# Attention beside a gated MLP in float32, one core: VectorE's low parts issued at the end of a step, and x prepared with longer distances

## The chip, the cores and the metric

The kernel runs on one core of a Trainium2 chip. A core has a matrix engine (PE, TensorE; its weight loads are listed apart as PEld), a vector engine (DVE, VectorE), a scalar engine (ACT, ScalarE), a general one (POOL, GpSimd), and SP, whose queue issues nearly all DMAs here. Each engine runs its own instructions in the order in which they are written; engines wait for each other by semaphores. The metric is the device time of one execution in microseconds (us). Before the change it was 1987.51 and 1981.97 us in two runs, with a median of 1984.74 us.

## The reference

```python
xn = layernorm(x)                                    # x: 2048 x 512
# A: attention, 32 heads of 128; the last 512 entries of the caches are used
q = xn @ wq                                          # 512 x 4096
p = softmax(q @ k^T * 128**-0.5)                     # 2048 x 512 for each head
s = concat(p @ v) @ wo                               # 4096 x 512
# B: gated MLP with a product over the sequence
z = gelu(xn @ w_in); z1, z2 = halves of z            # 688 columns each
g = silu((z1 * (w_sp @ layernorm(z2) + b_sp)) @ w_out)
out = x + s * g
```

Everything is float32. The kernel makes every product of two float32 matrices from three products of a rounded type: each operand is cut into a high part (a cast) and a low part (the operand minus its high part), and high x high, high x low and low x high are summed.

## The kernel before, in words

**Attention.** A block is one head times 512 rows of x; there are 128 blocks of 4 steps each, so 512 steps (`NSTEP`), and step `t` handles 128 rows. Around step `t` the main loop writes, for several blocks at once, a software pipeline:

- `score(t)`: three matmuls into a PSUM tile of 512 columns (`ps_3`, four buffers, shared with `outp`), its row maximum on DVE (`nm`, L439) and the exponential on ACT (`prob`, L441);
- `turn(t-1)`: DVE turns 32 x 32 blocks of `prob` (`pB`, L449), and SP stores the result to `p_dram`. After four of them `turned` reads them back in turned order as `pL`;
- `shares(t-10)`: the high part of P^T on ACT (`pT_h`, L466), its low part on POOL (`pT_l`);
- `pv(t-12)`: three matmuls of P and V. After the fourth of a block, `pv_out` makes `oT_h` on ACT and `oT_l` on DVE;
- `outp(t-17)`: three matmuls with wo, added to the rows' sums by DVE (`sacc`, L494);
- two or three of 42 matmuls per 16 steps that make q for the next four blocks (L413). They are seven products in the manner of Strassen, on quarters of 256 columns. `q_sum` forms sums of weights on POOL; `q_split` makes the high part on ACT (L395) and the low part on POOL for three of the seven and on DVE for four. High and low part go to a ring of four entries (`wring`, an `x8` tile, shown as x). `q_evict` and `q_done` take the results from PSUM, and `q_out` makes `qT_h` and `qT_l`.

**x.** The second half of the rows is prepared while the first is worked on. `later_x(p)` for p = 0 to 3 loads two tiles of 128 rows (`rawx`, five buffers), normalises them on DVE (`ln_stats`, `ln_apply`), turns them on PE, and makes eight pieces of 256 columns: four quarters and four sums of quarters (`T1` to `T4`). Of each, ACT makes the high and DVE or POOL the low part, and SP stores both to `x_dram` (`part`, L269). `fetch_x` reads them back before they are needed, as eight transfers of 1 MB. `t_sums` and `t_split` do the same for the first half in the steps -3 to 1.

**Order.** The order is the order of the program, written out by the main loop; nothing is reordered. Within a step it is: the loads due; `shares`; what the table `todo` has for this step (`plan`'s weight pieces, `q_sum` and `q_split`, `later_x`); `score`; the q products; `pv`; `outp`; `q_events` (`q_evict`, `q_done`); `pv_out`; `turned`; `turn`; and what `ends` has. So DVE's part of a step reads: low parts of `q_split` and `part`, `nm`, `sacc`, then `qs` and `qT_l` where due, `oT_l` where due, `pB`. The helper `rest` writes all low parts, which is why they share the line L59:

```python
def rest(engine, lo, whole, hi):
    engine.tensor_tensor(lo, whole, hi.bitcast(F32), op=OP.subtract)
...
for n, f in enumerate(f for p in range(4) for f in later_x(p)):
    at(30 + 5 * n // 2, f)
```

The last two lines put the 18 entries of each `later_x(p)` into `todo`, five steps for two entries, from step 30 to step 207. After the attention come the z products, layernorm, and the product over the sequence with the output (about the last 380 us of the span).

Of the kernel before, what the change touches and what calls it, by code (L numbers as in the profile page):

```python
# [8 lines left out]
F32 = mybir.dt.float32  # L9
# [3 lines left out]
OP = mybir.AluOpType  # L13
# [27 lines left out]
def mixer_kernel(ctx: ExitStack, tc: tile.TileContext, x, wh, w_in, w_sp, b_sp, w_out, out):  # L41
# [16 lines left out]
    def rest(engine, lo, whole, hi):  # L58
        engine.tensor_tensor(lo, whole, hi.bitcast(F32), op=OP.subtract)  # L59

# [160 lines left out]

    def t_sums(p):
# [27 lines left out]
    def later_x(p):  # L250
# [13 lines left out]
        def part(k, src, engine):  # L264
            st = xq.tile([P, 512], F32R, name="rawx")
            hi, lo = st[:, :256], st[:, 256:]
            nc.scalar.copy(hi, src())
            rest(engine, lo, src(), hi)
            nc.sync.dma_start(xd[1, k][:, :, :, p * P:(p + 1) * P],  # L269
                              st.bitcast(F32).rearrange("p (a c q) -> p a c q", a=2, q=P))  # L270
# [7 lines left out]
        def new_sums():  # L278
# [4 lines left out]
        vec, gp = nc.vector, nc.gpsimd  # L283
        return [load,
                lambda: ln_stats([t[a], t[b]], 100 * (p + 1)),
                lambda: ln_apply(t[a], 100 * (p + 1)),
                lambda: ln_apply(t[b], 100 * (p + 1) + 1),
                lambda: turned_copy(a),
                lambda: turned_copy(b),
                new_sums,  # L290
                lambda: part((0, 0), half(a, 0), vec),
                lambda: sub(half("u", 1)(), half(b, 1)(), half("u", 0)()),
                lambda: part((0, 1), half(b, 0), vec),
                lambda: part((1, 0), half(a, 1), gp),
                lambda: sub(half(b, 0)(), half(b, 1)(), half(b, 0)()),
                lambda: part((1, 1), half(b, 1), vec),
                lambda: sub(half(a, 1)(), half(a, 1)(), half("u", 1)()),
                lambda: part("T1", half("u", 0), gp),
                lambda: part("T2", half("u", 1), vec),
                lambda: part("T3", half(b, 0), gp),  # L300
# [655 lines left out]
```

## Time and profile before

| | |
|---|---|
| Time, median of two runs | 1984.74 us |
| The profiled execution's own time | 1983.97 us |
| Its span on the core | 1982.1 us |
| Mean granted TensorE clock | 0.986 |
| Busy: PE, DVE, POOL, ACT | 94%, 75%, 64%, 59% |
| HBM traffic over the span | 216 GB/s |

Rows of the profile that group instructions read: line, engine, operation, output<-inputs with the program's names (buffer numbers left out, so `ps_3` is ps), shapes and count | busy us in total, mean ns of one | idle time of the engine just before them in us, and what ended most of it. Rows of a timeline begin with the start and the duration in us and may end in square brackets with the idle time before them. A row of waits reads: who, waited for whom: us in total, times, longest. Rows of windows give the window's length, then busy us and instructions of PE, PEld, DVE, ACT and POOL, then the granted clock, the mean busy share of the 16 DMA engines, and GB/s.

### The profile page before, as it was taken

How to read it: one execution, taken by the hardware profiler on the slowest of the kernel's cores; microseconds unless marked ns; L12 is line 12 of the kernel's file. 1: busy time of each engine (PE TensorE's matmuls, PEld its weight loads, DVE VectorE, ACT ScalarE, POOL GpSimd, SP SyncE). 2: the span in 40 equal slices, each digit the busy share in tenths (PEclk: the TensorE clock that was granted, in tenths of full speed). 3: DMA queues.
4: the chain of work that ended last, by engine and by line, in shares of the span. 5: the costliest groups of instructions: out<-in, count | busy, mean ns of one | idle time of the engine just before them, and what ended most of it. 6: DMA issues, size and time to landing. Idle time of an engine off the chain costs nothing.

```text
span 1982.1 us, 28951 instructions
## 1 busy us (share of the span) xinstructions
PE 1860.5 (94%) x8658; PEld 1537.5 (78%) x8658; DVE 1484.3 (75%) x2427; ACT 1174.1 (59%) x2627; POOL 1264.1 (64%) x1127
## 2 busy tenths in 40 slices
PE   8888989989889899999999999999999999999999
PEld 7766767767667677677777777777777799999998
DVE  5678888888888788788888888888888756434333
ACT  4655656656666666666666666676666644334332
POOL 3576868878777787777888887888788626000000
PEclk9999999999999999999999999999999999999999
DMA  5698988988988899999989989989889961655442
GB/s 173 182 272 205 244 226 218 239 234 220 237 225 222 212 231 265 311 265 236 234 237 226 238 227 230 243 231 228 237 223 249 261 205 51 203 168 164 151 147 92
DMA packets 442542, 429.23 MB, mean 217 GB/s; under 512 B 26032, under 2 KB 318640, under 8 KB 440336
## 3 DMA queue, kind: packets, MB, share of 16 engines
q1 hardware_dynamic: 437776, 421.74, 79.0%
q10 hardware_dynamic: 4608, 5.64, 0.8%
q8 instruction: 68, 1.11, 0.2%
q14 instruction: 90, 0.74, 0.1%
HBM read 260.55 MB, written 166.72 MB: 216 GB/s over the span
## 4 chain that ended last, share of the span: by engine, by line
PE 36%; ACT 20%; DVE 17%; DMA 11%; issue 10%; POOL 4%; SPq 1%; ACTq 0%; DVEq 0%; POOLq 0%
ACT prob L441 8%; DVE nm L439 6%; ACT pT_h L466 4%; DMA pL<-p_dram 4%; PE ps_g L64 4%; PE ps_g L63 4%; PE ps_g L65 4%; DVE pB L449 4%; PE ps L63 3%; PE ps L65 3%; PE ps L64 3%; PE ps_a L413 3%; PE ps_a L64 3%; PE ps_a L63 3%; PE ps_a L65 3%
## 5 line engine op out<-in xcount | busy, mean ns | idle before, releaser
L59 POOL TENSOR_TENSOR pT_l<-pL,pT_h 128x512 fp32r<-128x512 f32 x507 | 670.7, 1323 | 266.9 <-ACT pT_h L466 244.5
L441 ACT ACTIVATE prob<-ps,nm 128x512 f32<-128x512 f32 x512 | 352.7, 689 | 504.0 <-DVE nm L439 502.7
L413 PE MATMUL ps_a<-x,x 128*128 128x512 f32 x1302 | 383.5, 395 | 0.5 <-DVE oT_l L59 0.3
L494 DVE SCALAR_TENSOR_TENSOR sacc<-ps,sums,sacc 128x512 f32<-128x512 f32 x496 | 363.4, 733 | 17.7 <-PE ps L65 16.6
L449 DVE STREAM_TRANSPOSE pB<-prob 128x512 f32<-128x512 f32 x512 | 357.4, 698 | 10.0 <-DMA p_dram<-pB 8.3
L439 DVE TENSOR_REDUCE nm<-ps 128x1 f32<-128x512 f32 x512 | 337.1, 658 | 3.1 <-PE ps L65 3.0
L466 ACT CAST pT_h<-pL 128x512 fp32r<-128x512 f32 x512 | 317.3, 620 | 23.7 <-DMA pL<-p_dram 10.6
L63 PE MATMUL ps<-wh,qT_h 128*128 128x512 f32 x512 | 221.8, 433 | 97.5 <-DVE sacc L494 92.3
L413 PEld LDWEIGHTS ps_a<-x,x 128*128 128x128 f32 x1302 | 247.7, 190 | 57.0 <-DVE oT_l L59 1.9
L59 POOL TENSOR_TENSOR wl<-raw,wh 128x512 fp32r<-128x512 f32 x192 | 251.6, 1311 | 8.7 <-ACT wh L139 8.7
L63 PEld LDWEIGHTS ps<-wh,qT_h 128*128 128x128 f32 x512 | 96.6, 189 | 180.6 <-DVE sacc L494 155.9
L64 PE MATMUL ps_a<-pT_l,wh 128*128 128x512 f32 x512 | 203.0, 397 | 4.0 <-POOL pT_l L59 3.9
L63 PE MATMUL ps_a<-pT_h,wh 128*128 128x512 f32 x512 | 202.1, 395 | 2.0 <-ACT pT_h L466 2.0
L65 PE MATMUL ps<-wh,qT_l 128*128 128x512 f32 x512 | 202.4, 395 | 0.0
L64 PE MATMUL ps<-wl,qT_h 128*128 128x512 f32 x512 | 202.3, 395 | 0.0
L63 PE MATMUL ps<-wh,oT_h 128*128 128x512 f32 x512 | 200.9, 392 | 0.7 <-DVE sacc L494 0.6
L65 PE MATMUL ps_a<-pT_h,wl 128*128 128x512 f32 x512 | 201.3, 393 | 0.0
L64 PE MATMUL ps<-wl,oT_h 128*128 128x512 f32 x512 | 200.0, 391 | 0.0
L65 PE MATMUL ps<-wh,oT_l 128*128 128x512 f32 x512 | 199.7, 390 | 0.0
L63 PE MATMUL ps_g<-z_h,x 128*128 128x344 f32 x512 | 162.2, 317 | 0.5 <-ACT z L719 0.5
L64 PE MATMUL ps_g<-z_l,x 128*128 128x344 f32 x512 | 162.1, 317 | 0.4 <-POOL z_l L59 0.4
L65 PE MATMUL ps_g<-z_h,x 128*128 128x344 f32 x512 | 161.9, 316 | 0.0
(197 smaller groups left out, 3342.6 us busy)
## 6 DMA issues: line engine op xcount, KB each, us to landing
p_dram<-pB SPq DMA_DIRECT2D x512, 256.0 KB, 5.1
pL<-p_dram SPq DMA_DIRECT2D x512, 256.0 KB, 5.6
raw<-wh SPq DMA_DIRECT2D x194, 256.0 KB, 5.0
wq<-wh SPq DMA_DIRECT2D x62, 256.0 KB, 6.2
x<-w_sp SPq DMA_DIRECT2D x60, 256.0 KB, 5.8
x<-x_dram SPq DMA_DIRECT2D x12, 1024.0 KB, 8.0
x_dram<-rawx SPq DMA_DIRECT2D x32, 256.0 KB, 4.0
u_dram<-uB SPq DMA_DIRECT2D x15, 384.0 KB, 2.3
```

The source lines that it names most:

```text
L59: engine.tensor_tensor(lo, whole, hi.bitcast(F32), op=OP.subtract)
L63: nc.tensor.matmul(ps, lh, rh, start=first, stop=False)
L64: nc.tensor.matmul(ps, lh, rl, start=False, stop=False)
L65: nc.tensor.matmul(ps, ll, rh, start=False, stop=last)
L413: nc.tensor.matmul(qps[g, bank], wt["q", g, k][a][:, c * P:(c + 1) * P], X[g * 2 // H][ORDER[k]][:, b, c], start=first, stop=r == 5, skip_ ...
L439: nc.vector.tensor_reduce(nm, ps, axis=AX.X, op=OP.max, negate=True)
L441: nc.scalar.activation(prob[t], ps, AF.Exp, bias=nm, accum_out=sums[b][:, j:j + 1])
L449: nc.vector.transpose(pB.rearrange("p (k q) -> p k q", q=Q), prob.pop(t))
L466: nc.scalar.copy(h, p)
L494: nc.vector.scalar_tensor_tensor(at, ps, rs, at, op0=OP.mult, op1=OP.add)
```

## The change

Three things change. First, the main loop gets a list `late`, which it works off at the end of a step, behind `turn(t-1)` and ahead of `ends`. The low parts that VectorE makes in `q_split`, in `part`, in `t_split`, in `q_out` (with scale) and in `pv_out` are put there instead of being written at once; the casts on ScalarE stay where they were. Second, those of 256 columns are written by `rest1`, as (a*1)-b, a scalar_tensor_tensor, in place of a tensor_tensor. Third, `later_x` becomes a sequence of 22 entries rather than 18: three empty ones stand between the load and the statistics, the store of a piece is an entry of its own one or more entries after the piece, and entries are 11/5 steps apart rather than 5/2, so that the whole runs from step 30 to step 221. VectorE and POOL now make four low parts each per p (before: five and three). In `t_sums` the last of four operations moves to the start of `t_split`, one step later.

```diff
+    def rest1(lo, whole, hi):
+        nc.vector.scalar_tensor_tensor(lo, whole, 1.0, hi.bitcast(F32), op0=OP.mult, op1=OP.subtract)
+
+    late = []
...
     def t_sums(p):
...
-        nc.vector.tensor_tensor(y[:, 256:], ps[:, 256:], o[:, 256:], op=OP.subtract)
+        t_ps[p] = ps
 
     def t_split(p):
         y, o = sacc[:, 4 + p, :], sacc[:, p, :]
+        nc.vector.tensor_tensor(y[:, 256:], t_ps.pop(p)[:, 256:], o[:, 256:], op=OP.subtract)
         for k, (name, src) in enumerate((("T2", o[:, 256:]), ("T1", o[:, :256]), ("T3", y[:, :256]), ("T4", y[:, 256:]))):
             hi, lo = (quarter(X[0][name][:, a], p) for a in range(2))
             nc.scalar.copy(hi, halves(src))
-            rest(nc.vector if k % 2 else nc.gpsimd, lo, halves(src), hi)
+            if k % 2:
+                late.append((rest1, lo, halves(src), hi))
+            else:
+                rest(nc.gpsimd, lo, halves(src), hi)
...
-        def part(k, src, engine):
-            st = xq.tile([P, 512], F32R, name="rawx")
+        def part(k, src, vector):
+            st = t[k] = xq.tile([P, 512], F32R, name="rawx")
             hi, lo = st[:, :256], st[:, 256:]
             nc.scalar.copy(hi, src())
-            rest(engine, lo, src(), hi)
+            if vector:
+                late.append((rest1, lo, src(), hi))
+            else:
+                rest(nc.gpsimd, lo, src(), hi)
+
+        def store(k):
             nc.sync.dma_start(xd[1, k][:, :, :, p * P:(p + 1) * P],
-                              st.bitcast(F32).rearrange("p (a c q) -> p a c q", a=2, q=P))
+                              t[k].bitcast(F32).rearrange("p (a c q) -> p a c q", a=2, q=P))
...
-        return [load,
-                lambda: ln_stats([t[a], t[b]], 100 * (p + 1)),
...
+        seq = [load, None, None, None,
+               lambda: ln_stats([t[a], t[b]], 100 * (p + 1)),
...
+               lambda: part((0, 0), half(a, 0), True),
+               lambda: sub(half("u", 1)(), half(b, 1)(), half("u", 0)()),
+               lambda: part((0, 1), half(b, 0), False),
+               lambda: part((1, 0), half(a, 1), True),
+               lambda: sub(half(b, 0)(), half(b, 1)(), half(b, 0)()),
+               lambda: part((1, 1), half(b, 1), False),
+               lambda: sub(half(a, 1)(), half(a, 1)(), half("u", 1)()),
+               lambda: part("T1", half("u", 0), True),
+               lambda: part("T2", half("u", 1), False),
+               lambda: part("T3", half(b, 0), True),
+               lambda: part("T4", half(a, 1), False)]
+        stores = {11: (0, 0), 13: (0, 1), 14: (1, 0), 16: (1, 1), 18: "T1", 19: "T2", 20: "T3", 21: "T4"}
+        return [(f, stores.get(n)) for n, f in enumerate(seq + [None])], store
...
         if scale:
             nc.scalar.activation(hi, ps, AF.Copy, scale=SCALE)
-            engine.scalar_tensor_tensor(lo, ps, SCALE, hi.bitcast(F32), op0=OP.mult, op1=OP.subtract)
+            late.append((nc.vector.scalar_tensor_tensor, lo, ps, SCALE, hi.bitcast(F32), OP.mult, OP.subtract))
...
         nc.scalar.copy(hi, src)
-        rest(nc.gpsimd if k in (0, 1, 5) else nc.vector, lo, src, hi)
+        if k in (0, 1, 5):
+            rest(nc.gpsimd, lo, src, hi)
+        else:
+            late.append((rest1, lo, src, hi))
         wt["q", g, k] = (hi, lo)
...
             nc.scalar.copy(hi, ps)
-            rest(nc.vector, lo, ps, hi)
+            late.append((rest, nc.vector, lo, ps, hi))
             oT[b] = (hi, lo)
...
-    for n, f in enumerate(f for p in range(4) for f in later_x(p)):
-        at(30 + 5 * n // 2, f)
+    n = 0
+    for p in range(4):
+        seq, store = later_x(p)
+        for f, k in seq:
+            t = 30 + 11 * n // 5
+            if f:
+                at(t, f)
+            if k is not None:
+                at(t, store, k)
+            n += 1
...
             turn(t - 1)
+        while late:
+            f, *args = late.pop(0)
+            f(*args)
         for f, *args in ends.get(t, ()):
             f(*args)
```

Two places show how the order moves. The first is on DVE in the middle of the main loop, a step in which `q_split`'s fourth piece (x<-wqs), a q eviction (qs) and an `oT_l` fall together, and the step after it. Before:

```order
L59 TENSOR_TENSOR x8_739<-wqs_8417,x8_739 128x256
L439 TENSOR_REDUCE nm_8735<-ps_3_8731 128x1
L494 SCALAR_TENSOR_TENSOR sacc_97<-ps_3_8745,sums_8079,sacc_97 128x512
L423 SCALAR_TENSOR_TENSOR qs_8679<-ps_a_8669,qs_8679 128x512
L59 TENSOR_TENSOR oT_l_8752<-ps_a_8635,oT_h_8751 128x512
L449 STREAM_TRANSPOSE pB_8755<-prob_8701 128x512
L439 TENSOR_REDUCE nm_8771<-ps_3_8766 128x1
```

And in the changed kernel (L62 is `rest1`, L459, L514, L443 and L469 are the old L439, L494, L423 and L449):

```order
L459 TENSOR_REDUCE nm_8734<-ps_3_8730 128x1
L514 SCALAR_TENSOR_TENSOR sacc_97<-ps_3_8744,sums_8065,sacc_97 128x512
L443 SCALAR_TENSOR_TENSOR qs_8678<-ps_a_8668,qs_8678 128x512
L469 STREAM_TRANSPOSE pB_8753<-prob_8701 128x512
L62 SCALAR_TENSOR_TENSOR x8_739<-wqs_8417,x8_739 128x256
L59 TENSOR_TENSOR oT_l_8751<-ps_a_8635,oT_h_8750 128x512
L459 TENSOR_REDUCE nm_8771<-ps_3_8766 128x1
```

The low part of x<-wqs moved from ahead of its step's `nm` to behind its `pB`, three to four instructions later, and `oT_l` from ahead of `pB` to behind it.

The second place is SP's queue during `later_x(0)`, around the store of its piece `T1` (x_dram15). Before:

```order
L452 DMA p_dram_2710<-pB_2785 128x512
L100 DMA raw_2788<-wh 128x512
L452 DMA p_dram_2710<-pB_2817 128x512
L269 DMA x_dram15_107<-rawx_2826 512x1x128
L452 DMA p_dram_2855<-pB_2853 128x512
```

In the changed kernel (L285, L472 and L105 are the old L269, L452 and L100):

```order
L472 DMA p_dram_2851<-pB_2883 128x512
L472 DMA p_dram_2851<-pB_2918 128x512
L472 DMA p_dram_2851<-pB_2956 128x512
L105 DMA raw_2961<-wh 128x512
L285 DMA x_dram15_107<-rawx_2894 512x1x128
L472 DMA p_dram_2995<-pB_2993 128x512
```

The numbers rise in the order in which the tiles are made. Before, the store follows the making of its piece at once (rawx_2826 lies between pB_2817 and pB_2853); now two P stores, of pB_2918 and pB_2956, stand between the piece (rawx_2894) and its store.

More of the change, by code (lines that the diff above doesn't have):

```diff
@@ L220, in mixer_kernel @@
     TS = ("T2", "T1", "T3", "T4")
+    t_ps = {}
     def t_sums(p):
@@ L282, in later_x @@
         a, b = ab
[L283 to L301 removed]
+        seq = [load, None, None, None,
+               lambda: ln_stats([t[a], t[b]], 100 * (p + 1)),
+               lambda: ln_apply(t[a], 100 * (p + 1)),
+               lambda: ln_apply(t[b], 100 * (p + 1) + 1),
+               lambda: turned_copy(a),
+               lambda: turned_copy(b),
+               new_sums,
+               lambda: part((0, 0), half(a, 0), True),
[11 more added lines that the diff above has]
+        return [(f, stores.get(n)) for n, f in enumerate(seq + [None])], store
     def zmm(ps, i, n, cs):
```

1 line of the change is left out of this document (removed).

## The prediction

> **What bounds the kernel now.** I read the page for the engines' shares, then busy time by windows, then the groups of DVE in one window, then who waits. The two groups of the page with PE's longest idle time, and two rows of waits:
>
> ```profile
> L63 PE MATMUL ps<-wh,qT_h 128*128 128x512 f32 x512 | 221.8, 433 | 97.5 <-DVE sacc L494 92.3
> L63 PEld LDWEIGHTS ps<-wh,qT_h 128*128 128x128 f32 x512 | 96.6, 189 | 180.6 <-DVE sacc L494 155.9
> ...
> PEld ps L63 <- DVE sacc L494: 159.1, 177, 6.5
> ...
> ACT prob L441 <- DVE nm L439: 502.7, 328, 7.3
> ```
>
> PE has one notable wait: the first matmul of `score` needs a PSUM tile that `sacc` must have read. Its weight load is held 159.1 us in all. ACT waits for DVE too, 502.7 us. So both hang on DVE, although the page calls DVE 75% busy. By windows (a stretch of plain steps, the stretch with `later_x`, and what follows the attention):
>
> ```profile
> 1030.00:1460.00 430.00, 413.83 (x1763) 326.51 (x1762) 371.75 (x607) 291.92 (x682) 352.15 (x307) 1.00 0.91 232
> 150.00:710.00 560.00, 501.60 (x2085) 391.04 (x2086) 469.76 (x754) 355.55 (x835) 435.50 (x389) 0.97 0.88 226
> 1600.00:1982.00 382.00, 377.03 (x2317) 364.55 (x2315) 165.24 (x279) 143.29 (x214) 42.18 (x40) 1.00 0.44 144
> ```
>
> In the plain stretch DVE is busy 371.75 of 430 us. Its groups there, by shape:
>
> ```profile
> L494 DVE SCALAR_TENSOR_TENSOR sacc<-ps,sums,sacc 128x512 f32<-128x512 f32 x152 | 111.3, 732 | 0.5
> ...
> L439 DVE TENSOR_REDUCE nm<-ps 128x1 f32<-128x512 f32 x152 | 99.8, 657 | 0.0
> L59 DVE TENSOR_TENSOR x<-wq,x 128x256 fp32r<-128x256 f32 x28 | 29.7, 1062 | 16.0 <-ACT x L395 16.0
> L59 DVE TENSOR_TENSOR oT_l<-ps_a,oT_h 128x512 fp32r<-128x512 f32 x38 | 26.3, 692 | 26.5 <-ACT oT_h L480 25.3
> ...
> L59 DVE TENSOR_TENSOR x<-wqs,x 128x256 fp32r<-128x256 f32 x9 | 7.8, 864 | 7.1 <-ACT x L395 7.1
> L347 DVE SCALAR_TENSOR_TENSOR qT_l<-ps_a,qT_h 128x512 fp32r<-128x512 f32 x10 | 6.9, 692 | 8.2 <-POOL pT_l L59 4.9 <-ACT qT_h L346 3.3
> ```
>
> The idle times are 0.5 + 16.0 + 26.5 + 7.1 + 8.2 = 58.3 us, and 371.75 + 58.3 is 430.05: DVE is never free, it works or stands before a low part whose cast is late. 152 `nm` in 430 us make 2.829 us a step, of which work 371.75/152 = 2.446 and standing 0.384. **DVE sets the pace of the plain steps.**
>
> What PE needs by itself comes from two `score` starts with 11 matmuls from one to the next and no wait between:
>
> ```profile
> 802.84 0.39 PE L63 MATMUL ps<-wh,qT_h 128*128 128x512 f32 x1
> ...
> 805.33 0.39 PE L63 MATMUL ps<-wh,qT_h 128*128 128x512 f32 x1
> ```
>
> 2.49/11 = 0.2264 us a matmul; a step has 9 + 42/16 = 11.625, so PE's floor is 2.632 us. The loop's length:
>
> ```profile
> L439 DVE TENSOR_REDUCE nm<-ps x512: 641/652/692, 55.4 to 1575.5; 128x1 f32<-128x512 f32 x171
> ```
>
> 1520.1 us for 511 steps. At 2.829 they would take 1445.6, so 74.5 us are extra. The groups of DVE in the second window that only `later_x` has:
>
> ```profile
> L59 DVE TENSOR_TENSOR rawx<-rawx 128x256 fp32r<-128x256 f32 x20 | 25.4, 1268 | 10.7 <-ACT rawx L267 8.1 <-POOL wq L386 1.3 <-POOL qT_l L59 1.2
> ...
> L187 DVE SCALAR_TENSOR_TENSOR rawx<-rawx,mv,rs_r 128x512 f32<-128x512 f32 x8 | 7.6, 948 | 0.0
> ...
> L171 DVE BATCH_NORM_STATS2 stt<-rawx 128x6 f32<-128x512 f32 x8 | 5.4, 680 | 8.7 <-DMA rawx<-x 8.6
> L172 DVE BATCH_NORM_AGGREGATE mv<-stt 128x2 f32<-128x6 f32 x8 | 1.5, 182 | 0.3
> ```
>
> Work 39.9 and idle 19.7, together 59.6 us, lengthen the loop. The other 14.9 I leave to the eight 1 MB fetches and the start. Behind 1600 us PE is busy 377 of 382, and nothing there changes.
>
> **The change part by part.** *Low parts of the ring (x<-wq, x<-wqs).* Their 23.1 us of standing end if they start later than the casts by more than now. They move behind `nm`, `sacc` and `pB`, some 2 us of DVE's work, and the cast keeps its place; at most a wait or two remains. *`oT_l` and `qT_l`* move behind `pB` alone. One such place:
>
> ```profile
> 1122.37 0.61 ACT L349 CAST qT_h<-qs 128x512 fp32r<-128x512 f32 x1
> 1122.88 0.59 ACT L480 CAST oT_h<-ps_a 128x512 fp32r<-128x512 f32 x1
> ...
> 1123.50 0.69 DVE L59 TENSOR_TENSOR oT_l<-ps_a,oT_h 128x512 fp32r<-128x512 f32 x1 [1.25 <-ACT oT_h L480]
> 1124.11 0.70 DVE L449 STREAM_TRANSPOSE pB<-prob 128x512 f32<-128x512 f32 x1
> ```
>
> `pB` needs nothing from the late cast and fills 0.62 of the 1.25 us; 0.63 stays. Over 38 waits of 0.70 on average I keep 9 of 26.5 us, and none of `qT_l`'s 8.2, together 0.06 us a step. DVE then needs 2.446 + 0.06 = 2.51 us, below PE's 2.632. Even if `oT_l` kept its whole 26.5 us (0.174 a step), DVE's 2.62 would still be below. **PE becomes the bound of the plain steps.** I take 2.67, a fifth of the way from 2.632 back to 2.829, for steps in which several low parts fall together.
>
> The consumers: a ring entry is first multiplied two or more steps after its split, and `oT_l` two steps later; one step of this is given up. Behind a late low part on DVE stands the next `nm`, for which ACT waits; that was so before.
>
> *(a\*1)-b.* Its nearest row is `sacc`, 0.732 us against 0.692 for a tensor_tensor of 512 columns: at most 0.04 dearer, 0.01 a step. The other end is 0.42, if the form kept clear of POOL, against 1.062 now: 0.16 a step cheaper. The rows of the old scalar_tensor_tensor with two inputs in SBUF decide it:
>
> ```profile
> 159.10 1.29 POOL L59 TENSOR_TENSOR pT_l<-pL,pT_h 128x512 fp32r<-128x512 f32 x1
> 159.49 1.45 DVE L187 SCALAR_TENSOR_TENSOR rawx<-rawx,mv,rs_r 128x512 f32<-128x512 f32 x1
> ...
> 584.60 0.70 DVE L187 SCALAR_TENSOR_TENSOR rawx<-rawx,mv,rs_r 128x512 f32<-128x512 f32 x1
> ```
>
> 0.70 us with POOL idle, 1.45 when a POOL instruction was under way, ending 0.55 after POOL's end. So this form waits for POOL as the other does, and I take no difference.
>
> The Trainium skill, "SBUF — State Buffer", section "Who interferes with whom", says the same: a VectorE instruction with two SBUF inputs contends with a GpSimd instruction that reads SBUF, the second to issue blocks until the first ends, and the operation does not matter. The rows above agree. By this rule the new form gains nothing; were it to escape, only the stretch of `later_x` below would gain, some 15 us.
>
> *`later_x`.* Sixteen low parts at about 1.06 in place of twenty at 1.27 are 17.0 us, and with 7.6 + 5.4 + 1.5 the work is 31.5; the idle 19.7 goes, since three entries (6.6 steps) follow the loads. Over 194 steps this is 0.16 a step; DVE needs 2.51 + 0.16 = 2.67, equal to PE's floor and a little over. Two engines that are both full disturb each other: I take 2.75. On SP, the queue that also stores P, two waits should go:
>
> ```profile
> SPq L269 <- POOL rawx L59: 25.3, 11, 4.1
> SPq L269 <- DVE rawx L59: 19.2, 15, 3.6
> ```
>
> They delay P stores for which PE waits only ten steps later, so I count nothing; if that cover is gone, they are in the 15 us of a rival below. POOL gets four low parts more, about 3 us of its 560. The moved operation of `t_sums` is four instructions at the start: nothing, within 3 us either way.
>
> **Sum.** 317 x 2.67 + 194 x 2.75 + 14.9 = 846.4 + 533.5 + 14.9 = 1394.8 us, against 1520.1: 125.3 us less. From the profiled execution's 1983.97 (0.8 below the median of the runs) this gives **1859 us**. With all steps at PE's floor it would be 1359.9 for the loop and 1824 in all.
>
> **Rivals.** *DMA takes the place of DVE.* The DMA engines' share of 0.91 at 2.829 us is 2.57 us of packets a step, and in the `later_x` stretch 0.88 x 560/177 = 2.78. If that share were a hard limit, the stretch could not go below 2.78, and the P tiles would come late elsewhere.
>
> ```profile
> p_dram<-pB SPq DMA_DIRECT2D x512, 256.0 KB, 5.1
> pL<-p_dram SPq DMA_DIRECT2D x512, 256.0 KB, 5.6
> ...
> ACT pT_h L466 <- DMA pL<-p_dram: 10.6, 9, 2.4
> ```
>
> Write and read back take 10.7 us of the six steps (17.0 us now, 16.0 then) between `pB` and `pT_h`, and there is little waiting yet. With 2.75 and 2.85 the loop is 871.8 + 552.9 + 14.9 = 1439.6, the whole 1903 us. Against it speaks that the share is of packets' time, which can shrink.
>
> *The change doesn't do what it says.* The standing moves: ACT, itself behind, hands the casts over later, or the P path holds everything at today's step. Only the idle time of `later_x` goes, 19.7 and perhaps 15 us of SP's: 1950 to 1984. Against it: ACT is busy 291.92 of 430 and waits for `nm`.
>
> *Slower: the low parts starve behind POOL.* There is a row for it:
>
> ```profile
> 255.53 1.31 POOL L59 TENSOR_TENSOR pT_l<-pL,pT_h 128x512 fp32r<-128x512 f32 x1
> 256.02 4.25 DVE L59 TENSOR_TENSOR rawx<-rawx 128x256 fp32r<-128x256 f32 x1 [1.19 <-POOL qT_l L59]
> 256.77 0.76 POOL L59 TENSOR_TENSOR x<-wq,x 128x256 fp32r<-128x256 f32 x1
> ...
> 258.70 1.29 POOL L59 TENSOR_TENSOR wl<-raw,wh 128x512 fp32r<-128x512 f32 x1
> ```
>
> DVE's instruction sat 4.25 us until POOL's run of instructions without a gap had ended, and the next `nm` behind it. POOL is busy 352 of 430 us, 2.32 a step; at 2.67 that is 87% and the gaps are fewer. A ring part comes every fourth step: DVE passes today's 2.829 once such a part takes 1.06 + (2.829 - 2.51)/0.25 = 2.34 us on average. At 3.5 us a step needs 2.51 + 0.25 x 2.44 = 3.12, the loop 511 x 3.12 + (16 x 3.5 + 14.5) + 14.9 = 1680 us, the whole 2144. Against it: the mean of 28 such parts now is 1.062.
>
> By the page's rule this starving is a plain consequence, the loser blocking fully; it does not say who wins between two waiting engines, so its chance stays that of one row in many.
>
> **How the numbers follow.** PE's floor reached nearly everywhere, 1824 to 1885 us: 0.58, and 1859 is its time. DMA or a mixture of near-full engines in between, 1885 to 1944: 0.26. No gain to speak of, within 2% (a measurement of this kernel can tell little less than that from no change), 1944 to 2024: 0.09. Slower by more: 0.07. So faster 0.84, same 0.09, slower 0.07. The range starts just under PE's floor and reaches through most of the second case: 1820 to 1932.
>
> **What would show it.** Right: DVE's idle time before x<-wq near zero and before `oT_l` under half; PE's weight load waiting for `sacc` well under 60 us; 2.65 to 2.70 us a step in the plain stretch, and DVE idle there before `sacc`, waiting for PE; low parts of 256 columns still near 1 us. Wrong: a step of 2.75 and more with ACT's `pT_h` waiting for pL, or with POOL named before `pv`; low parts of 2 us and more; or the standing found again before `oT_l`.

## The result, and the profile after

The changed kernel takes 1879.65 us (median of 2 runs, 1877.79 to 1881.52), against 1984.74 before: 0.947 of it, 95% interval 0.940 to 0.954. The forecast was 1859, range 1820 to 1932. The profiled execution took 1881.52 us, 102.5 less than the 1983.97 of before, where the sum had 125.3. So the direction and most of the size are there, and some 23 us are missing. The rest of this text is about these 23 us, and about why what was gained was gained.

First the rows that answer those shown of before. From the page's groups, PE's first `score` matmul (L68, the old L63):

```profile
L68 PE MATMUL ps<-wh,qT_h 128*128 128x512 f32 x512 | 204.2, 399 | 23.0 <-DVE sacc L514 20.1
```

Three rows of the view of waits (us in all, times, longest):

```profile
PEld ps L68 <- DVE sacc L514: 28.7, 23, 4.1
...
ACT prob L461 <- DVE nm L459: 317.0, 315, 6.8
...
DVE sacc L514 <- PE ps L70: 79.1, 174, 2.2
```

PE stood 97.5 us before this matmul, and now 23.0; its weight load waited 159.1 us for `sacc`, and now 28.7. In its place a wait the other way round: DVE's `sacc` stands 79.1 us, 174 times, for PE's matmul (16.6 us and 19 times before). The row of before:

```profile
DVE sacc L494 <- PE ps L65: 16.6, 19, 1.9
```

The pace has passed from DVE to PE.

Busy time by windows, the plain steps as before, and the stretch that covers the entries of `later_x` as they lie now:

```profile
1030.00:1460.00 430.00, 423.77 (x1856) 348.03 (x1855) 390.95 (x640) 310.76 (x721) 365.48 (x319) 1.00 0.94 248
84.00:643.00 559.00, 534.41 (x2299) 432.46 (x2300) 508.50 (x818) 391.47 (x916) 476.85 (x429) 0.98 0.95 253
```

And DVE's groups in the plain window (L59 is still `rest`, L62 is `rest1`, L705 the end of the step, where the late list is worked off):

```profile
L514 DVE SCALAR_TENSOR_TENSOR sacc<-ps,sums,sacc 128x512 f32<-128x512 f32 x162 | 120.3, 743 | 27.7 <-PE ps L70 27.5
...
L459 DVE TENSOR_REDUCE nm<-ps 128x1 f32<-128x512 f32 x161 | 107.0, 665 | 1.1 <-PE ps L70 1.1
L62 DVE SCALAR_TENSOR_TENSOR x<-wq,x 128x256 fp32r<-128x256 f32 x28 | 29.3, 1045 | 0.0
L59 DVE TENSOR_TENSOR oT_l<-ps_a,oT_h 128x512 fp32r<-128x512 f32 x40 | 27.2, 679 | 7.4 <-ACT oT_h L500 6.7
...
L705 DVE SCALAR_TENSOR_TENSOR qT_l<-ps_a,qT_h 128x512 fp32r<-128x512 f32 x10 | 6.6, 665 | 0.3
L62 DVE SCALAR_TENSOR_TENSOR x<-wqs,x 128x256 fp32r<-128x256 f32 x9 | 6.5, 723 | 0.0
```

161 steps in 430 us are 2.671 us a step. The 16.0 and 7.1 us of standing before the ring's low parts (the x tiles) are 0.0, `oT_l` stands 7.4 us in place of 26.5, `qT_l` 0.3 in place of 8.2. What stands now is `sacc`, 27.7 us, and it stands for PE. Undisturbed, a step is shorter still, as a mean over the 16 steps in which the loop repeats itself (within these 16, steps differ, 1.9 to 4.7 us from `nm` to `nm`). Two `nm` of the timeline, 80 steps apart:

```profile
959.71 0.68 DVE L459 TENSOR_REDUCE nm<-ps 128x1 f32<-128x512 f32 x1
...
1170.51 0.68 DVE L459 TENSOR_REDUCE nm<-ps 128x1 f32<-128x512 f32 x1
```

210.8 us for 80 steps is 2.635, PE's floor (the estimate was 2.632), held for five groups of 16 in a row. The whole loop, by the start of its first and its last `nm`:

```profile
L459 DVE TENSOR_REDUCE nm<-ps x512: 643/672/692, 52.1 to 1473.1; 128x1 f32<-128x512 f32 x171
```

The transfers of P, from the page's list of DMA issues (the last column is the median us from issue to landing):

```profile
p_dram<-pB SPq DMA_DIRECT2D x512, 256.0 KB, 5.4
pL<-p_dram SPq DMA_DIRECT2D x512, 256.0 KB, 5.4
```

And the row of waits that goes with them:

```profile
ACT pT_h L486 <- DMA pL<-p_dram: 74.4, 42, 6.5
```

10.8 us for the way there and back, 10.7 before; but `pT_h` now waits 74.4 us for it, where it was 10.6. The loop takes 1421.0 us in place of 1520.1, and starts 3.3 us earlier: 102.4 us, the whole difference of the profiled executions. Behind it nothing changed. At 2.635 all 511 steps would take 1346.5, so 74.5 us are still extra. Part of them shows in a view that no mean of a group shows. The shortest, the median and the longest of each kind of DVE's 256-column low parts (ns, then the first and last start):

```profile
L62 DVE SCALAR_TENSOR_TENSOR x<-wq,x x93: 376/793/5035, 68.4 to 1423.5; 128x256 fp32r<-128x256 f32 x93
...
L62 DVE SCALAR_TENSOR_TENSOR rawx<-rawx x16: 382/836/7083, 198.3 to 673.8; 128x256 fp32r<-128x256 f32 x16
```

The same instruction takes 0.38 us or 7.08. The longest one, with DVE's timeline around it and then POOL's in the same stretch (start, duration):

```profile
237.20 0.65 DVE L459 TENSOR_REDUCE nm<-ps 128x1 f32<-128x512 f32 x1
...
238.89 0.70 DVE L469 STREAM_TRANSPOSE pB<-prob 128x512 f32<-128x512 f32 x1
239.51 7.08 DVE L62 SCALAR_TENSOR_TENSOR rawx<-rawx 128x256 fp32r<-128x256 f32 x1
246.52 0.68 DVE L59 TENSOR_TENSOR oT_l<-ps_a,oT_h 128x512 fp32r<-128x512 f32 x1
247.12 0.67 DVE L459 TENSOR_REDUCE nm<-ps 128x1 f32<-128x512 f32 x1
```

```profile
238.75 1.29 POOL L59 TENSOR_TENSOR pT_l<-pL,pT_h 128x512 fp32r<-128x512 f32 x1
240.00 0.74 POOL L59 TENSOR_TENSOR x<-wq,x 128x256 fp32r<-128x256 f32 x1
240.69 1.29 POOL L59 TENSOR_TENSOR pT_l<-pL,pT_h 128x512 fp32r<-128x512 f32 x1
241.94 1.26 POOL L59 TENSOR_TENSOR wl<-raw,wh 128x512 fp32r<-128x512 f32 x1
243.16 1.25 POOL L59 TENSOR_TENSOR pT_l<-pL,pT_h 128x512 fp32r<-128x512 f32 x1
244.37 1.26 POOL L59 TENSOR_TENSOR wl<-raw,wh 128x512 fp32r<-128x512 f32 x1
245.59 0.72 POOL L403 TENSOR_TENSOR wq<-wq 128x256 f32<-128x256 f32 x1
```

DVE's low part starts at 239.51 and ends at 246.59. In that time POOL ran seven instructions, each starting before the one ahead of it had ended; its last ends at 246.31, and DVE's 0.28 us later. From one `nm` to the next, 237.20 to 247.12, are 9.9 us. There are 12 such rows of over 2 us in the loop: seven of the ring (x<-wq), always in the sixth step of a group of 16 (t mod 16 = 5), and five of `rawx`. If the step that PE is in when such a row begins and the two behind it, taken on PE from `score` to `score`, are held against three times 2.635, they cost 42.6 of the 74.5 us (0.3 more or less, by which matmul of `score` one counts from). As steps differ, this count over three steps is rough; by whole groups of 16 the five rows of the last 255 steps cost 10.9 us, where it gives 9.7.

Part of this price is PE's clock, which stands at half for a while behind some of these stops. The window just behind the row of 7.08 us (granted clock third from the end):

```profile
246.60:253.40 6.80, 6.15 (x15) 4.80 (x16) 6.09 (x11) 5.05 (x12) 2.87 (x3) 0.50 0.47 135
```

In it matmuls of 512 columns start 0.427 us apart, elsewhere 0.227. The loop has seven such stretches of 3.4 or 6.8 us, 34.1 us in all, five of them right behind a long row; that is up to 17 us of PE's work, 13 of it inside the 42.6.

This starving is the mechanism of the third rival, the low parts that starve behind POOL, in 12 rows of 140.

So **theory 1**: the gain is the late low parts, which hand the pace to PE; what is missing is starving, and it can be had back by placing the low parts where POOL pauses. **The rival**: the transfers of P and the preparation's own work take the missing time, and the long rows only fill time that is lost anyway.

### The profile page after: what moved, and what is told of

Its sections match the earlier page's. It is cut to its first block, busy times and chain, and to the rows that moved or that the text cites. A ratio compares the mean times of both kernels' runs of the same rounds, so it can differ in the third digit from the quotient of the medians.

```text
span 1879.7 us, 28930 instructions
## 1 busy us (share of the span) xinstructions
PE 1819.2 (97%) x8658; PEld 1545.7 (82%) x8658; DVE 1482.9 (79%) x2423; ACT 1178.6 (63%) x2627; POOL 1258.3 (67%) x1131
## 4 chain that ended last, share of the span: by engine, by line
PE 76%; DVE 8%; DMA 6%; issue 4%; POOL 3%; ACT 2%; SPq 1%; ACTq 0%; POOLq 0%; DVEq 0%
PE ps_a L433 12%; PE ps L68 10%; PE ps L69 10%; PE ps L70 10%; PE ps_a L69 6%; PE ps_a L70 6%; PE ps_a L68 6%; PE ps_g L69 4%; PE ps_g L70 4%; PE ps_g L68 4%; DMA p_dram<-pB 3%; DMA pL<-p_dram 2%; DVE nm L459 2%; DVE sacc L514 2%; DVE pB L469 2%
## 5 line engine op out<-in xcount | busy, mean ns | idle before, releaser
L59 POOL TENSOR_TENSOR pT_l<-pL,pT_h 128x512 fp32r<-128x512 f32 x507 | 663.1, 1311 | 171.7 <-ACT pT_h L486 144.3
L514 DVE SCALAR_TENSOR_TENSOR sacc<-ps,sums,sacc 128x512 f32<-128x512 f32 x496 | 368.0, 742 | 80.8 <-PE ps L70 79.1
L469 DVE STREAM_TRANSPOSE pB<-prob 128x512 f32<-128x512 f32 x512 | 358.5, 700 | 33.4 <-DMA p_dram<-pB 30.9
L486 ACT CAST pT_h<-pL 128x512 fp32r<-128x512 f32 x512 | 317.0, 619 | 102.0 <-DMA pL<-p_dram 74.4
L459 DVE TENSOR_REDUCE nm<-ps 128x1 f32<-128x512 f32 x512 | 340.9, 666 | 6.1 <-PE ps L70 6.0
L59 POOL TENSOR_TENSOR wl<-raw,wh 128x512 fp32r<-128x512 f32 x192 | 249.7, 1301 | 8.8 <-ACT wh L144 8.8
L68 PE MATMUL ps<-wh,qT_h 128*128 128x512 f32 x512 | 204.2, 399 | 23.0 <-DVE sacc L514 20.1
L68 PE MATMUL ps_a<-pT_h,wh 128*128 128x512 f32 x512 | 201.5, 394 | 5.3 <-ACT pT_h L486 5.3
L68 PE MATMUL ps<-wh,oT_h 128*128 128x512 f32 x512 | 201.4, 393 | 0.0
L59 POOL TENSOR_TENSOR qT_l<-qs,qT_h 128x512 fp32r<-128x512 f32 x93 | 121.9, 1310 | 72.9 <-ACT qT_h L366 66.8
L68 PE MATMUL ps_g<-z_h,x 128*128 128x344 f32 x512 | 162.4, 317 | 0.5 <-ACT z L750 0.5
```

Source lines behind the costliest of these rows:

```text
L68: nc.tensor.matmul(ps, lh, rh, start=first, stop=False)
L459: nc.vector.tensor_reduce(nm, ps, axis=AX.X, op=OP.max, negate=True)
L469: nc.vector.transpose(pB.rearrange("p (k q) -> p k q", q=Q), prob.pop(t))
L486: nc.scalar.copy(h, p)
L514: nc.vector.scalar_tensor_tensor(at, ps, rs, at, op0=OP.mult, op1=OP.add)
```

## Experiments

Each run was timed beside runs of the kernel before on the same chip, whose median lay between 1985.88 and 1990.43 us in the three sets of runs; so ratios are compared. The column "long" counts DVE's 256-column low parts of over 2 us in the loop (ring, `rawx`); the last two columns are us from the 17th `nm` to the 225th, where the preparation lies, and from the 257th to the 512th, read from the timelines. These columns are of one execution each; the two of the changed kernel differ by 1.7 and by 7.7 us.

```
kernel                            us       ratio  95%              long    208 steps  255 steps
before (the profiled run)                                          2, 2    655.6      725.0
changed (the profiled run)                                         7, 5    597.8      686.8
changed, again        e7       1884.49   0.9488  0.9462-0.9514    8, 4    596.1      694.5
late list alone       e1       1897.77   0.9532  0.9510-0.9554    8, 0    611.1      688.6
ring alone late       e6       1935.02   0.9719  0.9705-0.9734    9, 2    628.6      703.5
preparation alone     e2       1992.37   1.0021  1.0007-1.0034    3, 4    660.3      725.2
  placed otherwise    e10      2009.18   1.0098  1.0076-1.0121    9, 0    677.2      729.7
plain a-b             e3       1890.23   0.9498  0.9484-0.9512    5, 5    604.6      687.2
one sum later         e5       1878.82   0.9461  0.9434-0.9488    3, 7    601.1      682.5
preparation placed    e8       1873.58   0.9435  0.9413-0.9457    10, 0   592.5      683.5
both of these         e9       1861.09   0.9368  0.9340-0.9396    4, 0    580.8      679.3
e9, one split later   e11      1867.08   0.9391  0.9367-0.9414    5, 0    585.6      683.0
three sums left out   e4       1859.67   0.9344  0.9320-0.9368    0, 1    583.3      676.0
no preparation        e12      1854.60   0.9310  0.9282-0.9338    13, 0   569.7      694.2
```

### Which part of the change brings the gain

**The late list alone (e1).** The kernel before, with the late list, and every low part of DVE put on it but those of `later_x`, which keep their old order, engines and distances:

```diff
+    def later(engine, *r):
+        if engine is nc.vector:
+            late.append((rest, engine, *r))
+        else:
+            rest(engine, *r)
...
-            rest(nc.vector, lo, ps, hi)
+            later(nc.vector, lo, ps, hi)
```

> The kernel before with the list alone: the low parts of the ring, of qT_l, of oT_l and of t_split go to the end of the step, still as a - b; the preparation of x is untouched. If DVE's standing before late casts set the pace (my theory), plain steps fall from 2.829 us to PE's floor of 2.63 to 2.68, the stretch of later_x stays DVE-bound at 2.51 + 0.33 = 2.84, and the time is 1880 to 1915 us. If the gain came from the longer distances in the preparation of x, plain steps stay near 2.83 and the time is over 1950. If it came from the form (a*1)-b, the same.

0.9532. The late list brings 4.7 of the 5.1 per cent by itself. The stretch of the preparation takes 611.1/208 = 2.94 us a step, where 2.84 was expected.

**The ring alone late (e6).** As e1, but only the pieces of `q_split` go on the list; `oT_l` and `qT_l` stay where they were:

```diff
-        rest(nc.gpsimd if k in (0, 1, 5) else nc.vector, lo, src, hi)
+        if k in (0, 1, 5):
+            rest(nc.gpsimd, lo, src, hi)
+        else:
+            late.append((rest, nc.vector, lo, src, hi))
```

> The kernel before with the low parts of the ring alone at the end of the step, as a - b; qT_l and oT_l stand where they stood. By my sum DVE then needs 2.446 + 0.174 + 0.05 = 2.67 us a step, just PE's floor or above: plain steps 2.66 to 2.70, the stretch of later_x about 2.95, the time 1895 to 1920 us. If oT_l's move were needed for most of the gain, plain steps stay at 2.75 or above and the time is over 1930.

0.9719, a little over half of the gain, and 15 us slower than the slow end expected. From DVE's groups in the plain window of this run:

```profile
L499 DVE SCALAR_TENSOR_TENSOR sacc<-ps,sums,sacc 128x512 f32<-128x512 f32 x158 | 116.7, 738 | 6.7 <-PE ps L67 5.8
L454 DVE STREAM_TRANSPOSE pB<-prob 128x512 f32<-128x512 f32 x158 | 110.7, 701 | 3.8 <-DMA p_dram<-pB 3.0 <-ACT pT_h L471 0.7
...
L59 DVE TENSOR_TENSOR x<-wq,x 128x256 fp32r<-128x256 f32 x30 | 29.9, 997 | 0.0
L59 DVE TENSOR_TENSOR oT_l<-ps_a,oT_h 128x512 fp32r<-128x512 f32 x40 | 27.7, 692 | 25.4 <-ACT oT_h L485 24.5
```

The ring's standing is gone, `oT_l`'s is whole, as intended. Counted on PE, the five groups of 16 steps that a long row falls in take 2.87 to 2.94 us a step. Of the ten without one, five run at 2.635 and five at 2.67 to 2.74. So the prediction's remark that PE would be the bound even with all of `oT_l`'s standing holds in a part of the groups only. By both signs set down beforehand (over 1930 us, 2.75 or more a step; the mean of the last 255 steps is 703.5/255 = 2.76) `oT_l`'s move is needed for most of the gain; by the ratios it is a little under half. In these 255 steps this kernel lost 703.5 - 255 x 2.635 = 31.6 us over the floor, e1 16.7. All that DVE does not spend waiting for PE or the P path is (430 - 6.7 - 3.8)/158 = 2.655 us a step: it has nothing free with which to make up what a long row delays. That this is the reason is argued from the rows, not tested by itself.

**The preparation alone (e2).** The changed kernel, with the late list replaced by one that carries out each entry at once:

```diff
-    late = []
+    class Now(list):
+        def append(self, x):
+            f, *args = x
+            f(*args)
+
+    late = Now()
```

> The changed kernel with nothing late: each low part is issued at once as before, but as (a*1)-b, and with the new preparation of x. My theory: plain steps stay at 2.83 us, since DVE stands before the same casts; only the idle time of later_x goes, some 20 to 35 us: 1945 to 1970 us. If distances or form make the gain: under 1920.

1.0021: nothing, where 20 to 45 us were expected. DVE's groups in the window 150 to 710 us, before and in e2, show the trade. `rawx` and `pB` before:

```profile
L449 DVE STREAM_TRANSPOSE pB<-prob 128x512 f32<-128x512 f32 x177 | 123.5, 698 | 2.5 <-DMA p_dram<-pB 2.5
...
L59 DVE TENSOR_TENSOR rawx<-rawx 128x256 fp32r<-128x256 f32 x20 | 25.4, 1268 | 10.7 <-ACT rawx L267 8.1 <-POOL wq L386 1.3 <-POOL qT_l L59 1.2
```

and in e2:

```profile
L474 DVE STREAM_TRANSPOSE pB<-prob 128x512 f32<-128x512 f32 x176 | 122.9, 699 | 9.5 <-ACT pT_h L491 5.6 <-DMA p_dram<-pB 3.8
...
L62 DVE SCALAR_TENSOR_TENSOR x<-wq,x 128x256 fp32r<-128x256 f32 x33 | 33.0, 999 | 18.8 <-ACT x L417 18.8
...
L62 DVE SCALAR_TENSOR_TENSOR rawx<-rawx 128x256 fp32r<-128x256 f32 x14 | 25.4, 1816 | 7.5 <-ACT rawx L283 6.1 <-POOL qT_l L59 1.2
...
L197 DVE SCALAR_TENSOR_TENSOR rawx<-rawx,mv,rs_r 128x512 f32<-128x512 f32 x8 | 9.5, 1186 | 0.0
```

The wait for the loaded rows (8.7 us before the statistics) did go. But fourteen low parts (two of the sixteen start behind this window) cost in busy time what twenty cost, 25.4 us, since each takes 1.82 us in place of 1.27, and 7.0 us of standing have come up before `pB`. Four of the 16 parts of `rawx` are long, 19.4 us together.

**Was it the placement of these long rows? (e10)** e2 with the entries of `later_x` at other steps, those of e8 below:

> Only the new preparation, nothing late (every low part at once), but its entries placed as in e8. Theory 1 (the preparation alone gained nothing because its parts were put where POOL runs without a gap): the five long rawx parts go, their 24 us over three steps each come back, steps 16 to 224 in 636 to 648 us in place of 659.5, whole 1965 to 1980 us. Rival (VectorE sets the pace at 2.83 us and its idle time only moves to pB and the ring): 650 us or more in these steps, whole 1983 to 1995 us.

1.0098, slower than before, and slower than both expectations; theory 1 was wrong on this. The long rows of `rawx` are gone, as it said. In DVE's groups of the same window:

```profile
L62 DVE SCALAR_TENSOR_TENSOR x<-wq,x 128x256 fp32r<-128x256 f32 x32 | 45.2, 1412 | 18.0 <-ACT x L417 18.0
...
L197 DVE SCALAR_TENSOR_TENSOR rawx<-rawx,mv,rs_r 128x512 f32<-128x512 f32 x8 | 14.1, 1765 | 0.0
...
L62 DVE SCALAR_TENSOR_TENSOR rawx<-rawx 128x256 fp32r<-128x256 f32 x14 | 12.3, 882 | 19.0 <-ACT rawx L283 13.8 <-issue 5.2
```

`rawx` saved 13.1 us of e2's busy time and took back 11.5 in standing; the ring's low parts became longer by 12.2 us, and the layer norm (L197, two SBUF inputs as well) by 4.6. These steps had been found by looking at the kernel with the late list; in one without it, POOL's instructions meet other ones of DVE. I read this so: as long as DVE sets the pace, moving the preparation only changes whom it meets. No further run tests it.

**The form (a\*1)-b (e3).** The changed kernel with `rest1` as a plain subtraction:

```diff
     def rest1(lo, whole, hi):
-        nc.vector.scalar_tensor_tensor(lo, whole, 1.0, hi.bitcast(F32), op0=OP.mult, op1=OP.subtract)
+        nc.vector.tensor_tensor(lo, whole, hi.bitcast(F32), op=OP.subtract)
```

> The changed kernel with a tensor_tensor in place of (a*1)-b. My theory (both forms have two inputs in SBUF and wait for POOL alike): the same within 0.7%, 1868 to 1893 us, with as many low parts of over 2 us as in the changed kernel (13). If the new form escapes POOL or starves more rarely: over 1900 us and more long rows. If the new form is the one that starves: under 1860 and few long rows.

0.9498, against 0.9471 and 0.9488 of the changed kernel in its two timings: within the intervals. The low parts have the same ends in both forms. Here, where those of the changed kernel stood above:

```profile
L62 DVE TENSOR_TENSOR x<-wq,x x93: 377/794/5025, 68.0 to 1431.4; 128x256 fp32r<-128x256 f32 x93
...
L62 DVE TENSOR_TENSOR rawx<-rawx x16: 388/949/7087, 197.0 to 680.1; 128x256 fp32r<-128x256 f32 x16
```

0.377 against 0.376 at the short end, 7.087 against 7.083 at the long one. Within these intervals, some 0.3%, the form neither costs nor escapes anything.

### Is it the starving that is missing?

One base and three placements ran together. **The base (e7)** is the changed kernel itself:

> The changed kernel again, as the base of the runs beside it. Both theories: 0.945 to 0.95 of the kernel before, 1877 to 1885 us; plain steps without a disturbance 2.635 us; some 12 low parts of over 2 us in the loop, always at the same steps (5 or 6 of each 16, and the third low part that VectorE makes for a stored block of x).

**One sum of POOL later (e5).** The fourth sum of each group of wq stood last in the run of POOL's instructions behind which the ring's low part starves; here it comes three steps later:

```diff
-        sums_at, splits_at = (-5, -4, -2, 1), (-3, -1, 2, 4, 6, 7, 10)
+        sums_at, splits_at = (-5, -4, -2, 4), (-3, -1, 2, 4, 6, 7, 10)
```

> One POOL sum (the fourth of each group of wq) three steps later, so that POOL has a pause at the step in which the ring's third low part falls. Theory 1 (the remaining loss in the plain steps is low parts that starve behind POOL's runs): of the 7 long ring parts at most 2 stay, those of rawx stay, and the three steps around each return 1.4 to 4.2 us: 12 to 15 us less than the changed kernel in the same call, ratio 0.992 to 0.994. Rival (the loss is DMA, the pL tiles and the stores of P that come late, and the long rows only fill time that is lost anyway): within 3 us.

5.7 us less than e7, where 12 to 15 were expected, with intervals that overlap. In steps 257 to 512, where only the ring has low parts of this shape, it is 682.5 against 694.5 us, the 12 us expected, with three long rows of the ring in place of eight; but against 686.8 of the changed kernel's other profile it is 4.3, so that this run alone doesn't show the size. In the stretch of the preparation 5.0 us were lost again: seven long parts of `rawx` in place of four.

**The preparation placed (e8).** The distances as a table, with period 48, so that DVE's low parts of `rawx` fall on steps where POOL had little behind it:

```diff
-            t = 30 + 11 * n // 5
...
+    AT = (0, 0, 0, 0, 7, 9, 11, 13, 15, 18, 24, 25, 23, 28, 27, 31, 30, 44, 39, 40, 43)
+    ST = {(0, 0): 27, (0, 1): 25, (1, 0): 31, (1, 1): 34, "T1": 47, "T2": 42, "T3": 43, "T4": 46}
...
+            at(30 + 48 * p + d, f, *args)
```

> The entries of the preparation of x at other steps, period 48, VectorE's low parts of rawx placed where POOL has little behind it. Theory 1: at most one long rawx part in place of five; the steps around these five are now 29 us longer than plain ones, so 15 to 29 us less than the changed kernel. Rival (DMA, the clock of 0.98 and the transposes set the length of this stretch): within 5 us.

10.9 us less than e7, under the 15 to 29 expected. No long part of `rawx` is left, but ten of the ring, 44.2 us of busy time in place of 35.7.

**Both (e9).**

> Both placements together. Theory 1: the gains add, 27 to 42 us less than the changed kernel, 1838 to 1855 us, and the steps between 256 and 511 at 2.64 on average. Rival (DMA): 1870 to 1885 us.

23.4 us less than e7, 1.2%, with intervals well apart (0.934 to 0.940 against 0.946 to 0.951): short of the 27 expected, and the fastest of the kernels that leave nothing out. Here the low parts are

```profile
L62 DVE SCALAR_TENSOR_TENSOR x<-wq,x x93: 379/792/4336, 68.7 to 1401.3; 128x256 fp32r<-128x256 f32 x93
...
L62 DVE SCALAR_TENSOR_TENSOR rawx<-rawx x16: 373/378/1084, 204.2 to 659.3; 128x256 fp32r<-128x256 f32 x16
```

with four long rows in place of twelve; by the count over three steps they cost 6.0 us, those of e7 38.6. The loop shortened by 31.8 us (1429.8 to 1398.0; e7's profiled execution was its slowest, 4.5 us over its median). So the starving was lost time, not a filling of time lost anyway. But the rival has its share: the stretch of the preparation takes 580.8 us, 548.1 of them floor and 3.3 long rows, so 29.4 are something else (in the two profiles of the changed kernel that remainder is 16.8 and 26.5). PE's longest waits in the loop of e9:

```profile
PE ps_a L68 <- ACT pT_h L486: 9.7, 6, 2.9
PE ps_a L69 <- POOL pT_l L59: 9.6, 15, 1.4
PE ps L68 <- DVE sacc L514: 7.1, 12, 1.1
```

First stands now the P path (`pT_h`, `pT_l`), which comes through the DMA.

**The ring's split one step later (e11)**, so that it falls behind the run:

```diff
-        sums_at, splits_at = (-5, -4, -2, 4), (-3, -1, 2, 4, 6, 7, 10)
+        sums_at, splits_at = (-5, -4, -2, 4), (-3, -1, 3, 4, 6, 7, 10)
```

> e9 with the ring's third split one step later, behind the two wl of POOL. Theory 1: the four long ring parts that were left go as well, 1.2 to 1.9 us each: 4 to 6 us less than e9, 1853 to 1859 us, steps 256 to 511 in 673 to 679 us. Rival: the low part meets POOL's next run, or comes late for its product: 1861 to 1868 us.

No gain (0.9391 against 0.9368, and the intervals overlap). Five long parts in the next step, and a wait of PE that e9 did not have at all:

```profile
PE ps_a L433 <- ACT x L412: 12.0, 12, 3.9
...
PE ps_a L433 <- DVE x L62: 6.5, 5, 2.2
```

The ring's entry now comes late for its product. That was the rival.

**Less work on POOL (e4).** Three of four sums a group are left out:

```diff
-        nc.gpsimd.tensor_tensor(to, x0, x1, op=op)
+        if k == 0:
+            nc.gpsimd.tensor_tensor(to, x0, x1, op=op)
```

> Three of POOL's four sums of wq a group are left out (the sums of the weights are not formed; the splits and products run on what is there): 0.72 us each, 2.2 of POOL's 37 us in 16 steps. Theory 1: POOL's run at steps 4 to 6 of each 16 ends one instruction earlier or breaks, at most 2 long ring parts of 7 or 8, those of rawx fewer or shorter; 1866 to 1876 us. Rival (the long parts come from something else than POOL's runs): the same number of long parts, 1880 to 1885 us.

0.9344, more than expected. Not one long part of the ring is left:

```profile
L62 DVE SCALAR_TENSOR_TENSOR x<-wq,x x93: 377/414/1424, 68.5 to 1399.3; 128x256 fp32r<-128x256 f32 x93
...
L62 DVE SCALAR_TENSOR_TENSOR rawx<-rawx x16: 377/528/4566, 198.2 to 658.6; 128x256 fp32r<-128x256 f32 x16
```

The median fell from 0.79 to 0.41 us and the longest from 5.04 to 1.42, and steps 257 to 512 take 676.0 us, 4.1 over the floor. Together with e5 this puts the cause on POOL's runs: the low part and its step are the same, only POOL's instructions are fewer.

**What the preparation costs now (e12).** All of it is left out:

```diff
-        nc.sync.dma_start(X[w][k].bitcast(F32), xd[w, k])
+        nc.sync.dma_start(X[w][k].bitcast(F32), xd[0, k if (0, k) in xd else (0, 0)])
...
-    for p in range(4):
+    for p in range(0):
```

> The preparation of x's second half is left out (no load, layer norm, transposes, sums, splits or stores of it; the later fetches read parts of the first half). It measures what the preparation costs in the changed kernel. By the prediction's term, 0.08 us on 194 steps, 15.5 us: 1864 to 1870 us. By theory 1 and the transposes, the five long parts (29 us), 32 transposes and their neighbours: steps 16 to 224 at 2.64 to 2.68, 549 to 557 us in place of 600, whole 1832 to 1842 us. The granted clock of 0.98 in this stretch, if the preparation has no part in it, stays.

0.9310, between the two. The stretch takes 569.7 us: 548.1 at the floor and, by the count over three steps, 20.5 of long rows leave 1.1. Without the preparation the ring starves more often (13 long rows), so that the difference of the two kernels shows less than the preparation's price. The mean clock in the window 84 to 643 us is 0.99 here, against 0.98 in the changed kernel. The preparation as such doesn't lower it: e9 has the preparation and 0.99 as well. Of the 208 steps, 27.3 us ran at half clock in the changed kernel (17.1 in e7), 13.7 in e9 and 13.7 here.

## Why the prediction was right, and where it was off

- **DVE sets the pace before, and what it stands for goes.** Right. The ring's 23.1 us of standing went to 0.0, `oT_l` kept 7.4 us (9 taken), `qT_l` 0.3 (none taken). DVE's need in the plain window is 390.95/161 = 2.428 us of work and (7.4 + 0.3)/161 = 0.048 of standing, 2.48 in place of the 2.51 worked out. e6 and e1 show both halves of it to be needed.
- **PE becomes the bound.** Right: 2.635 us where nothing disturbs, 2.671 as a mean of the window, 2.67 taken. DVE waits for PE 174 times.
- **The plain margin.** 0.035 us on every step was put down to several low parts falling together. The size was near, the cause was another: nine of the last ten groups of 16 steps without a long row have no margin at all when counted on PE, and a few long rows cost up to 4 us each. That the mean of the window came out as forecast is luck; the last 255 steps have 686.8/255 = 2.69.
- **`later_x`: 194 x 2.75.** This is the term that was mis-sized. On the 208 steps from the 17th to the 225th the sum had 194 x 2.75 + 14 x 2.67 = 570.9 us, 22.8 over the floor of 548.1. They took 597.8: 32.9 us of long rows by the count over three steps (28.8 of them `rawx`, 4.1 the ring), and 16.8 of all else, which is near the 15.5 that the preparation had been given (in e7 the two are 21.5 and 26.5, so this nearness is not to be built on). What failed is the step that put its low parts down "at about 1.06": they took 1.94 on average in the window 84 to 643 us,

```profile
L62 DVE SCALAR_TENSOR_TENSOR rawx<-rawx 128x256 fp32r<-128x256 f32 x14 | 27.2, 1942 | 0.0
```

  and a mean hides that one row of 7 us stops PE while fourteen of 1 us would not. The idle 19.7 us of this stretch did not simply "go" either: e2 shows them coming back as longer low parts and as standing before `pB` as long as DVE is the bound.
- **The other pieces of the loop.** The last 255 steps 686.8 in place of 680.9; the first 16 and the 32 with the fetches 136.5 in place of 143.0. With +26.9 for the preparation this is 26.3 too long, less the 3.3 us by which the loop starts earlier: the 23 us that are missing.
- **(a\*1)-b costs and gains nothing.** Right, by e3. The Trainium skill, "SBUF — State Buffer", section "Who interferes with whom", says that the shape of the operation doesn't decide; the trace agrees, 0.376 and 0.377 us at the short end, 7.08 and 7.09 at the long one.
- **The rival "DMA takes the place of DVE"**: not as a limit. The share rose to 0.94 at 2.671 us, 2.51 us of packets a step where it was 2.57. As a second cause it is there: `pT_h` waits 74.4 us for pL in place of 10.6, and once the starving is gone (e9) the P path is PE's longest wait.
- **The rival "low parts starve behind POOL"**: its mechanism came, its size did not. It needed a mean of 2.34 us to end slower; the ring's mean is 1.045. Its chance of 0.07 was that of "slower", and the prediction had no term for a few such rows, although before's own trace had four of over 2 us. Its signs pointed both ways: "near 1 us" held for the mean, "2 us and more" for 12 rows.
- **SP's waits counted at nothing.** They went: the two rows have 44.5 us before and 42.5 in e1, 0.7 in the changed kernel and none in e2. In e2, where DVE sets the pace, nothing was gained in all; what it is worth with PE as the bound, no run here tells apart from the rest.

## What to carry to other kernels

When the engine that sets the pace stands before instructions whose inputs are late, issuing these behind its urgent work gives the standing back, until the next engine's floor; what that floor is, the closest pair of its own starts tells. A change to an engine that is off the new bound (the preparation here) may be worth nothing by itself and some half a per cent with the other (0.9532 against 0.9488, intervals that just touch). Don't take the mean of a group for the price of one: read shortest, median and longest, and where the longest is ten times the shortest, look up which steps they fall on and move those few, or break up the other engine's run behind which they stand.

## What the runs showed of the hardware

- **A DVE instruction with two inputs in SBUF can be passed over, not only held up.** At 239.51 us it stood behind one POOL instruction that had 0.53 us to go; six more POOL instructions that started later, at 240.00 and after, ran ahead of it. It got through only when POOL had a pause. POOL's own instructions in that run took their usual 0.72 to 1.29 us. The Trainium skill, in the same section of "SBUF — State Buffer", says that issue order decides who blocks; these rows differ from it.
- **It happened where POOL's run was long already.** In the changed kernel's profile, 48 of the 140 low parts start beside a POOL instruction that the next one follows without a gap (within 0.03 us). 36 of the 48 got through right behind that one instruction, and it was POOL's next that waited: those of 512 columns took 1.47 to 1.52 us, 1.30 is usual. So it was at the place of before that the prediction shows, where DVE's row of 159.49 us ended at 160.94 and POOL's next row is

```profile
160.34 1.74 POOL L59 TENSOR_TENSOR wl<-raw,wh 128x512 fp32r<-128x512 f32 x1
```

  The other twelve were passed over by two to six. For all twelve, 14 to 19 POOL instructions had by then followed each other without a gap; for 34 of the 36 it was 1 to 10, for two 18 and 19. Over the fourteen profiles, 121 of the 127 that were passed over had 12 or more, 738 of the 759 that got through 11 or fewer. Why the length of the run decides is not shown.
- **Those with one input in SBUF were not held up.** The same low part takes 0.38 us when POOL is idle (28 rows, 0.38 to 0.41). At 238.89 `pB`, one input in SBUF, took 0.70 us beside a POOL instruction that had started 0.14 us earlier; all 512 `pB` took 0.69 to 0.71 us, all 128 `oT_l`, whose other input is in PSUM, 0.65 to 0.69.
- **The long rows are not the same from run to run.** The same kernel, profiled twice, had seven and eight long parts of the ring and five and four of `rawx`, the ring's partly in other groups of 16 steps but always in the same step of the group; so a kernel's loss to them differs by some 4 us (42.6 and 38.6) without any change.
- **PE's granted clock halves behind a stop of some us, and not each time.** All seven stretches at half clock in the changed kernel's loop come within 5 us of a place where PE's matmuls start 2.0 to 5.2 us apart. They last 3.4 or 6.8 us. Seven of the twelve long rows have none behind them.
